# A first softmax rearranged: v transposed under the exponentials, and the A^T W products split into halves by softmax column block

## The chip, the cores and the metric

The kernel runs on one core of one Trainium2 chip. The metric is the device time of one execution in microseconds (us). A kernel is timed in several executions, interleaved with executions of the kernel before on the same chip.

Names in the profiles: PE is TensorE's matmuls, PEld its weight loads, DVE is VectorE, ACT ScalarE, POOL GpSimd, SP SyncE; L282 is line 282 of that kernel. `x6` counts instructions; what stands in square brackets is the idle time of the engine before them, and what ended it.

## The reference, cut to what matters

```python
def _attn_ref(q, k, v, tau):            # q, k, v: 4 x 6144 x 256
    qn = q / (norm(q, axis=1) + 1e-06)  # over the 6144 rows
    kn = k / (norm(k, axis=1) + 1e-06)
    s = kn.transpose(0, 2, 1) @ qn / tau      # 256 x 256 per batch
    a = softmax(s, axis=-1)
    return v @ a
def _moe_ref(x, w1, w2, w3, w_out):     # x: 24576 x 256, w1..w3: 256 x 768, w_out: 768 x 256
    h = np.maximum(np.maximum(x @ w1, x @ w2), x @ w3)
    return h @ w_out
```

Since (v A) W = v (A W), the kernel multiplies the small softmax matrix into the three weights once per batch (tile `aw`; called the A^T W products here, because the softmax matrix lies transposed in memory), and v then meets only these: the h matmuls multiply v^T, v transposed, with them. It works on v in 48 chunks of 512 rows, 12 to a batch.

## The kernel before: the parts concerned

Everything below is about the first batch, before the stream of chunks can start. Its softmax is computed from the Gram products, the matmuls of k with q. The exponentials `et` come in two column blocks, j = 0 and j = 1, and each A^T W product is a sum over both. Row sums give the reciprocal `rinv`, which scales each product when ACT or DVE evicts it from PSUM (the matmul accumulator) to SBUF. `htile` takes one of six PSUM banks, `xtile` one of two.

```python
    ps = gram(0)
    warm_ps = htile("warm_ps")
    for i in range(8):                       # keeps TensorE busy while DVE and ACT work
        PE.matmul(warm_ps, lhsT=ident, rhs=warm, start=(i == 0), stop=(i == 7))
    et = softmax_t(*ps)
    aw = alloc_aw()
    rinv = rowsums(et)                       # 4 tiny matmuls, then DVE.reciprocal
    v_transpose_pe(0)                        # 8 PE transposes, ACT's copy, DVE's copy
    aw_part(et, rinv, aw, 0, FT)             # 12 products, 6 evictions
    ...
    def aw_part(et, rinv, aw, fp, w):
        for m in range(3):                   # the three weights
            for ic in range(CC):
                ew = htile("ew_ps")
                for j in range(CC):
                    PE.matmul(ew[:, :w], lhsT=et[:, j, ic * P:(ic + 1) * P], rhs=w_sb[m][:, j, fsl], ...)
                # evicted by ACT and DVE in turn, times rinv
    ...
    load_v(0)                                # queued behind the k and q loads
    for fp in range(d_ff // FT):
        load_w(fp)                           # block 0 of w1, w2, w3, then block 1, then block 2
```

A helper at the end pins the program's order on each engine, so each engine executes in the order of the source.

## Time and profile before

| | us |
|---|---|
| time, median of three runs | 576.76 |
| TensorE busy, of a span of 574.9 | 555.1 |
| the stretch that the change touches (end of the Gram products to the products of the second weight block) | 34.05 to 39.61 |
| TensorE's gaps after 39.61, up to 570 | none |

The prediction shows the lines for these.

### The profile page before, as it was taken

How to read it: one execution, taken by the hardware profiler on the slowest of the kernel's cores; microseconds unless marked ns; L12 is line 12 of the kernel's file. 1: busy time of each engine (PE TensorE's matmuls, PEld its weight loads, DVE VectorE, ACT ScalarE, POOL GpSimd, SP SyncE). 2: the span in 40 equal slices, each digit the busy share in tenths (PEclk: the TensorE clock that was granted, in tenths of full speed). 3: DMA queues.
4: the chain of work that ended last, by engine and by line, in shares of the span. 5: the costliest groups of instructions: out<-in, count | busy, mean ns of one | idle time of the engine just before them, and what ended most of it. 6: DMA issues, size and time to landing. Idle time of an engine off the chain costs nothing.

```text
span 574.9 us, 9325 instructions
## 1 busy us (share of the span) xinstructions
PE 555.1 (97%) x3328; PEld 328.5 (57%) x3328; DVE 406.4 (71%) x627; ACT 307.2 (53%) x530; POOL 227.3 (40%) x235
## 2 busy tenths in 40 slices
PE   3789999999999999999999999999999999999996
PEld 3655555555755555555575555555575555555554
DVE  0048777777577777777748777777848778778774
ACT  1034567677454466776735447767646444444442
POOL 4232257776731028777761006777760000000000
PEclk9999999999999999999999999999999999999999
DMA  9998998885598228977378526788535234322111
GB/s 142 107 144 157 130 178 124 157 133 113 102 118 164 59 66 155 133 152 130 75 131 130 114 75 101 157 131 130 125 84 127 66 82 129 74 91 76 56 73 74
DMA packets 75951, 65.62 MB, mean 114 GB/s; under 512 B 52353, under 2 KB 61953, under 8 KB 75905
## 3 DMA queue, kind: packets, MB, share of 16 engines
q0 software_dynamic: 18928, 26.48, 39.1%
q1 hardware_dynamic: 56832, 38.28, 22.9%
q8 instruction: 26, 0.43, 0.3%
q10 hardware_dynamic: 144, 0.26, 0.1%
q14 instruction: 21, 0.16, 0.1%
HBM read 78.64 MB, written 25.17 MB: 181 GB/s over the span
## 4 chain that ended last, share of the span: by engine, by line
PE 93%; DMA 5%; ACT 0%; DVE 0%; issue 0%; POOL 0%; DVEq 0%; POOLq 0%
PE h_ps L327 65%; PE o_ps L346 21%; DMA q_sb<-in_q_dram 4%; PE gram L235 3%; PE ew_ps L282 3%; DMA k_sb<-in_k_dram 2%; PE o_ps L366 0%; PE gram L178 0%; PE n_ps L216 0%; PE n_ps L218 0%; ACT et L246 0%; PE gram L180 0%; DVE o_sb L372 0%; POOL k_sb L99 0%; DVE scr L253 0%
## 5 line engine op out<-in xcount | busy, mean ns | idle before, releaser
L327 PE MATMUL h_ps<-vt_sb,aw_sb 128*128 128x512 bf16 x1728 | 406.6, 379 | 0.0
L331 DVE TENSOR_TENSOR s_mx<-h_ps,s_mx 128x512 bf16<-128x512 f32 x288 | 197.9, 687 | 98.1 <-ACT s_mx L330 97.1
L327 PEld LDWEIGHTS <-aw_sb 128*128 128x128 bf16 x1728 | 168.2, 98 | 163.0 <-DVE aw_sb L288 3.7
L330 ACT ACTIVATE s_mx<-h_ps 128x512 bf16<-128x512 f32 x288 | 171.4, 595 | 130.7 <-PE h_ps L327 130.7
L332 DVE TENSOR_TENSOR ht_sb<-h_ps,s_mx 128x512 bf16<-128x512 f32 x288 | 199.2, 692 | 30.7 <-PE o_ps L346 0.5
L204 POOL TENSOR_TENSOR acc<-acc,sq 128x768 f32<-128x768 f32 x90 | 147.7, 1651 | 70.7 <-ACT sq L198 70.5
L346 PE MATMUL o_ps<-wo_sb,ht_sb 128*128 128x256 bf16 x1128 | 153.9, 273 | 0.0
L346 PEld LDWEIGHTS <-ht_sb 128*128 128x128 bf16 x1128 | 110.4, 98 | 52.9
L349 ACT ACTIVATE o_sb<-o_ps 128x512 f32<-128x512 f32 x94 | 56.1, 597 | 83.1 <-PE o_ps L346 83.1
L110 POOL DMA_DIRECT2D v_sb<-in_v_dram x48 | 26.8, 562 | 88.5 <-DMA vt_sb<-v_sb 86.6
L198 ACT ACTIVATE sq<-q_sb 128x768 bf16<-128x768 fp8e4 x48 | 40.5, 844 | 0.0
L198 ACT ACTIVATE sq<-k_sb 128x768 bf16<-128x768 fp8e4 x48 | 40.1, 835 | 0.0
L201 POOL CAST acc<-sq 128x768 f32<-128x768 bf16 x6 | 4.9, 821 | 64.6 <-ACT sq L198 64.6
L102 POOL DMA_DIRECT2D q_sb<-in_q_dram x32 | 17.7, 555 | 10.7 <-DMA k_sb<-in_k_dram 9.7
L166 PE MATMUL kk<-k_sb 128*128 128x256 fp8e4 x48 | 7.8, 339 | 11.7 <-DVE k_sb L152 5.4
L285 ACT ACTIVATE aw_sb<-ew_ps,rinv 128x384 bf16<-128x384 f32 (+1 forms) x27 | 14.4, 546 | 5.7 <-PE ew_ps L282 4.8
L282 PE MATMUL ew_ps<-w_sb,et 128*128 128x384 bf16 (+1 forms) x108 | 17.1, 308 | 0.0
L235 PE MATMUL gram<-k_sb,q_sb 128*128 128x512 fp8e4 x144 | 16.8, 277 | 0.0
L99 POOL DMA_DIRECT2D k_sb<-in_k_dram x29 | 16.0, 554 | 1.0 <-POOLq L462 0.8
L235 PEld LDWEIGHTS <-q_sb 128*128 128x256 fp8e4 x144 | 15.9, 136 | 0.6
L178 PE MATMUL gram<-k_sb,q_sb 128*128 128x512 fp8e4 x48 | 10.7, 323 | 3.4 <-DMA q_sb<-in_q_dram 3.4
L166 PEld LDWEIGHTS <-k_sb 128*128 128x256 fp8e4 x48 | 6.5, 182 | 12.8 <-DMA k_sb<-in_k_dram 6.3
(52 smaller groups left out, 103.6 us busy)
## 6 DMA issues: line engine op xcount, KB each, us to landing
out_dram<-o_sb SPq DMA_DIRECT2D x47, 512.0 KB, 2.8
v_sb<-in_v_dram POOLq DMA_DIRECT2D x48, 256.0 KB, 3.7
k_sb<-in_k_dram POOLq DMA_DIRECT2D x24, 192.0 KB, 5.3
q_sb<-in_q_dram POOLq DMA_DIRECT2D x24, 192.0 KB, 6.8
k_sb<-in_k_dram POOLq DMA_DIRECT2D x5, 256.0 KB, 10.8
q_sb<-in_q_dram POOLq DMA_DIRECT2D x5, 256.0 KB, 19.4
w_sb<-in_moe_w_dram POOLq DMA_DIRECT2D x9, 128.0 KB, 5.7
kf<-in_k_dram SPq DMA_DIRECT2D x2, 512.0 KB, 4.3
```

The lines of the kernel that those rows point to most:

```text
L102: POOL.dma_start(out=qk[b][0][:, g0:g0 + w, :], in_=q_r[b][:, g0:g0 + w, :])
L110: POOL.dma_start(out=t, in_=v_r[gi // NCH, gi % NCH])
L198: ACT.activation(out=sq, in_=src, func=AF.Square)
L204: POOL.tensor_tensor(out=acc, in0=acc, in1=sq, op=ALU.add)
L235: PE.matmul(g[:, j * C:(j + 1) * C], lhsT=qt[:, tsl, j * P:(j + 1) * P], rhs=kt[:, tsl, :], start=(tp == 0 and j == 0), stop=(tp == NG // ...
L282: PE.matmul(ew[:, :w], lhsT=et[:, j, ic * P:(ic + 1) * P], rhs=w_sb[m][:, j, fsl], start=(j == 0), stop=(j == CC - 1))
L327: PE.matmul(t.rearrange("p (t n) -> p t n", t=TPC), lhsT=aw[m][:, ic, fsl], rhs=vt[:, :, ic, :], start=(ic == 0), stop=(ic == CC - 1))
L330: ACT.activation(out=s_mx, in_=hp[0], func=AF.Copy)
L331: DVE.tensor_tensor(out=s_mx, in0=hp[1], in1=s_mx, op=ALU.max)
L332: DVE.tensor_tensor(out=ht[:, fc, :], in0=hp[2], in1=s_mx, op=ALU.max)
L346: PE.matmul(st["ps"][:, half], lhsT=ht[:, fc, t * P:(t + 1) * P], rhs=wo_sb[:, fc, :], start=(fc == 0), stop=(fc == FC - 1))
L349: ACT.activation(out=st["o"][:, t - 1:t + 1, :].rearrange("p t d -> p (t d)"), in_=st["ps"], func=AF.Copy)
```

## The change

The intent: transposes need only v, so they can run while ACT computes the exponentials; and the first half of every product needs only the first exponential, so it can run while ACT computes the second.

```diff
+    def aw_first(et, aw):
+        ...
+        products(0)              # j = 0: six products, two for each weight
+        sums(0)
+        sums(1)
+        DVE.reciprocal(out=rinv, in_=rs_ps[:, 0:CC])
+        products(1)              # j = 1: six products
+        # six evictions, ACT and DVE in turn, as before
...
+        DVE.tensor_copy(out=vt[:, half:, :], in_=ps[:, half:, :])
         ACT.activation(out=vt[:, :half, :], in_=ps[:, :half, :], func=AF.Copy)
-        DVE.tensor_copy(out=vt[:, half:, :], in_=ps[:, half:, :])
...
-    for i in range(8):
-        PE.matmul(warm_ps, lhsT=ident, rhs=warm, start=(i == 0), stop=(i == 7))
+    for i in range(6):
+        PE.matmul(warm_ps, lhsT=ident, rhs=warm, start=(i == 0), stop=(i == 5))
     et = softmax_t(*ps)
+    v_transpose_pe(0)
     aw = alloc_aw()
-    rinv = rowsums(et)
-    v_transpose_pe(0)
-    aw_part(et, rinv, aw, 0, FT)
+    rinv = aw_first(et, aw)
```

More of the change, by code (lines that the diff above doesn't have):

```diff
@@ L290, in aw_part, with sums, products @@
                 n += 1
+    def aw_first(et, aw):
+        rinv = sm.tile([P, CC], FP32, name="rinv")
+        rs_ps = xtile("rs_ps")
+        parts = [(m, ic, htile("ew_ps")) for m in range(3) for ic in range(CC)]
+        def sums(j):
+            for ic in range(CC):
+                PE.matmul(rs_ps[:, ic:ic + 1], lhsT=et[:, j, ic * P:(ic + 1) * P], rhs=ones_c,
+                          start=(ic == 0 and j == 0), stop=(j == CC - 1), skip_group_check=True)
+        def products(j):
+            for m, ic, ew in parts:
+                PE.matmul(ew[:, :FT], lhsT=et[:, j, ic * P:(ic + 1) * P], rhs=w_sb[m][:, j, 0:FT],
+                          start=(j == 0), stop=(j == CC - 1))
+        products(0)
[3 more added lines that the diff above has]
+        products(1)
+        for n, (m, ic, ew) in enumerate(parts):
+            if n % 2 == 0:
+                ACT.activation(out=aw[m][:, ic, 0:FT], in_=ew[:, :FT], func=AF.Copy, scale=rinv[:, ic:ic + 1])
+            else:
+                DVE.tensor_scalar_mul(out=aw[m][:, ic, 0:FT], in0=ew[:, :FT], scalar1=rinv[:, ic:ic + 1])
+        return rinv
     vts = {}
```

## The prediction

> **What bounds the kernel now.** I read the page first: its busy shares, then the chain that ended last.
>
> ```profile
> PE 555.1 (97%) x3328; PEld 328.5 (57%) x3328; DVE 406.4 (71%) x627; ACT 307.2 (53%) x530; POOL 227.3 (40%) x235
> ...
> PE 93%; DMA 5%; ACT 0%; DVE 0%; issue 0%; POOL 0%; DVEq 0%; POOLq 0%
> ```
>
> TensorE is 93% of the chain, the opening loads another 5%. Second I cut the span into stretches at the points that the change touches (columns: stretch, its length, busy time and instructions of PE, PEld, DVE, ACT, POOL; clock; DMA share and GB/s).
>
> ```profile
> 0.00:34.05 34.05, 19.01 (x147) 17.13 (x147) 1.63 (x6) 3.14 (x4) 13.17 (x27) 1.00 1.01 126
> 34.05:39.61 5.56, 5.32 (x40) 2.96 (x39) 3.06 (x12) 3.60 (x9) 2.39 (x4) 1.00 1.44 194
> 39.61:51.44 11.83, 11.83 (x68) 6.44 (x66) 11.09 (x20) 6.88 (x13) 3.18 (x6) 1.00 0.68 109
> 51.44:570.00 518.56, 518.56 (x3077) 301.83 (x3076) 389.93 (x590) 292.99 (x503) 208.54 (x199) 1.00 0.59 113
> ```
>
> Up to 34.05 us the Gram products wait for q and k. From 39.61 us to 570 TensorE has no gap at all: 11.83 of 11.83 and 518.56 of 518.56 us. So only one thing can change: the moment, 39.61 us, at which TensorE has got through the first softmax and the first h block and goes on without a gap. All of the change is in the 5.56 us before it. Third, the timeline of that stretch (start, duration, engine, line, count):
>
> ```profile
> 34.05 1.90 PE L380 MATMUL warm_ps<-warm,ident 128*128 128x512 bf16 x8
> ...
> 35.33 0.91 ACT L246 ACTIVATE et<-e_in,rq 128x256 bf16<-128x256 f32 x2
> ...
> 36.29 0.23 PE L270 MATMUL rs_ps<-ones_c,et 128*128 128x1 bf16 x3 [0.22 <-ACT et L246]
> ...
> 36.38 0.61 PE L312 MATMUL vt_ps<-ident,v_sb 128*128 128x128 bf16 x8
> 36.55 0.17 DVE L272 RECIPROCAL rinv<-rs_ps 128x2 f32<-128x2 f32 x1 [1.06 <-PE rs_ps L270]
> ...
> 36.82 1.47 PE L282 MATMUL ew_ps<-w_sb,et 128*128 128x256 bf16 x12
> 37.02 0.60 ACT L316 ACTIVATE vt_sb<-vt_ps 128x512 bf16<-128x512 bf16 x1 [0.79 <-PE vt_ps L312]
> 37.52 1.20 ACT L285 ACTIVATE aw_sb<-ew_ps,rinv 128x256 bf16<-128x256 f32 x3
> 37.65 0.42 DVE L317 COPY vt_sb<-vt_ps 128x512 bf16<-128x512 bf16 x1 [0.93 <-ACT vt_sb L316]
> 37.99 1.26 DVE L288 TENSOR_SCALAR aw_sb<-ew_ps,rinv 128x256 bf16<-128x256 f32 x3
> ...
> 38.13 1.65 PE L327 MATMUL h_ps<-vt_sb,aw_sb 128*128 128x512 bf16 x6
> ```
>
> A group's duration holds a tail of its last matmul, so I use spacings: warm (1.90-0.38)/7 = 0.22 us, transposes (0.61-0.22)/7 = 0.056, A^T W products (1.47-0.27)/11 = 0.109. The six h matmuls would need 6 x 0.216 = 1.30 us; they take 39.61-38.13 = 1.48, because DVE's first product eviction comes late (37.99), behind its copy of v^T, which itself waited 0.93 us for ACT's copy.
>
> **What the Trainium skill says.** "PSUM — Partial Sum Buffer", section "PSUM bank collisions raise a hardware error", says two engines may not touch one bank in the same quadrant at once, ScalarE with VectorE reads included, so a scheduler orders them. The trace agrees: the two v^T copies read disjoint halves of one bank and run one after the other (0.60, then 0.42 us). Changing their order does not make them parallel. "TensorE: Matmul & The Clock Gate", section "Back-to-back issue gap", gives 262 cycles for 256 columns; at its 2.4 GHz that is 0.109 us, my spacing above. The same page, "What's actually happening" under Part 1, puts the throttle behind an idle window of some 3.4 us; the granted clock is 1.00 in every stretch above, and no gap that I work out below exceeds 0.5 us, so two warm matmuls less should not cost clock. "DMA: Bandwidth & Descriptors", section "Issuing engines are not separate DMA queues", says that all loads interleave on the same 16 DMA engines: so weights that are queued behind q cannot be hurried. The DMA share of 1.44 in the stretch agrees that these are full.
>
> **The change, part by part.**
> (a) Two warm matmuls go: TensorE is free of them at 34.05 + 6 x 0.216 = 35.35 instead of 35.78. This was time in which it waited for the exponentials anyway.
> (b) The eight transposes fill it: 35.35 to 35.79, results complete about 36.0. Their bank is free (the first e_in product ends about 35.16), and v landed about 20.89 + 13.8 = 34.7. They no longer stand, 0.44 us, between sums and products.
> (c) DVE copies its half at about 36.0 to 36.42, ACT its at 36.45 to 37.05. Before, this pair was over at 38.08, in the way of the evictions.
> (d) First-half products need only the first exponential. The first row sum before started at 35.89, just when that exponential was there; so do they now: weight 1 at 35.89 and 36.00, weight 2 at 36.11 and 36.22. Weight 3 would be due at 36.33. Here I looked at when the weights land; the issues of w1 to w3 start at 23.34, 25.80 and 28.25:
>
> ```profile
> 28.25 0.70 POOL L136 DMA_DIRECT2D w_sb<-in_moe_w_dram  x1 [1.73 <-DMA q_sb<-in_q_dram]
> ```
> ```profile
> w_sb<-in_moe_w_dram POOLq DMA_DIRECT2D x1, 128.0 KB, 8.4
> ```
>
> The same view, window by window, gives 12.0, 10.2 and 8.4 us to landing: 35.34, 36.00, 36.65. In the kernel before the third was not wanted until 36.82 + 8 x 0.109 = 37.69, a full 1.0 us of slack, so no wait shows. **In the changed kernel the third weight is wanted 0.32 us before it lands**, and everything behind it on the in-order TensorE (row sums, second half) waits. It starts about 0.05 us after landing, as the late Gram products did after their q (31.27 to 31.32 in the chain in order of time): 36.70 and 36.81, free at 36.92.
> (e) Four row sums, 0.03 us apart, complete about 37.17; the reciprocal, 0.17, at 37.21 to 37.38. It was done at 36.73 before: **the reciprocal comes 0.65 us later**. Second-half products issue at 37.02 to 37.68.
> (f) Evictions start at about 37.42 on both engines. From the rows above: ACT's come 0.36 us apart and last 0.48, DVE's 0.39 and 0.48. ACT ends at 37.90, 38.26, 38.62; DVE at 37.92, 38.31, 38.70.
> (g) h matmuls, each after its weights with 0.04 us for the semaphore, at least 0.216 apart: 37.94, 38.16, 38.37, 38.59, 38.80, 39.02; TensorE is free at 39.24. The evictions stay ahead, so 1.30 us, not 1.48.
> Sum: 39.61 - 39.24 = 0.37 us less. The six PSUM buffers serve as before, since the first h tiles take banks whose evictions they wait for anyway.
>
> **What becomes of it later.** TensorE has no gap after, so 0.37 us should reach the end, unless a load now comes late. The closest is the output weight: issued at 45.16, 5.2 us to landing, so 50.3; wanted at 51.44 before, at 51.07 after. Its issue hangs on the DMA transpose of the second v, which no moved instruction starts. 0.7 us of slack remain. The second column block of the weights lands by about 38.7 and is wanted at 39.24. So 576.76 - 0.37 = 576.4 us.
>
> **The rivals.**
> 1. *No wait for the third weight* (it lands earlier in the timed runs, or my landing sum is wrong). Then first halves are over at 36.55, the reciprocal at 37.0, evictions start at 37.08 (ACT is then held by its v^T copy), h at 37.60, free at 38.90: 0.71 us less, 576.05. Against it: three landings 0.66 us apart on full DMA engines, untouched by the change.
> 2. *The wait eats the gain*: were the weight 0.4 us later, near 37.05, all of (d) to (g) would slip by as much: 576.76, nothing won.
> 3. *Something later gives it back*: the output weight or a v transpose on the DMA queue becomes the wait. 0.7 us of slack speaks against it; it would make 576.7.
> 4. *The clock*: two warm matmuls less leave TensorE throttled. It has 1.00 and is not idle for long; a loss would be several us, 580. Very unlikely.
>
> **Range and chances.** The main line with small errors gives 576.2 to 576.6, the first rival 576.0, the second and third 576.8; the three runs before agree to the hundredth, so spread between runs adds little, a tenth or two. I take 575.8 to 576.9. Two per cent are 11.5 us, more than twice the whole 5.56 us stretch that is changed: faster than that is impossible by this route, slower only by a throttled clock.
>
> **What would show it right or wrong.** Right: in the changed profile TensorE's products show an idle of 0.3 to 0.5 us released by the load of w_sb, between the fourth and fifth; the reciprocal starts about 37.2; the first h matmul at 37.9 and the six without gaps; the next products at about 39.2; no gap after. Wrong: products run through from 35.9 (rival 1); h starts after 38.1 (rival 2); the first o_ps product (line 374 of the changed kernel) waits for wo_sb (rival 3); a granted clock below 1.00 (rival 4).

## More of the kernel before

Most fast runs of one kernel lie within a few tenths of a microsecond of each other; some, of 577.1 to 578.4 us, are longer and still count as fast.

One more view is needed for the comparison: the chain of work that ended last, in order of time (start, length, what). This is its part in the stretch:

```profile
35.33 0.92 ACT et L246 x2
...
36.29 0.23 PE rs_ps L270 x3
36.52 0.47 PE vt_ps L312 x8
36.98 1.31 PE ew_ps L282 x12
38.30 0.22 PE h_ps L327
38.51 0.01 issue
38.52 1.25 PE h_ps L327 x5
39.78 1.31 PE ew_ps L282 x12
```

Exponentials, row sums, transposes, products and h matmuls stand one behind another. The chain puts a matmul's end at the end of its pipeline; the timeline puts the start of the products that follow at 39.62. This start, "TensorE's next products" below, is the moment that each variant is judged by, because TensorE has no gap after it.

## The result and the profile after

The changed kernel took 576.55 us (median of six runs, 576.35 to 576.66), beside 576.80 for the kernel before (six runs, 576.76 to 576.92). The ratio is 0.9995, with a 95% interval of 0.9982 to 1.0008: the interval holds 1. Ratios here are over the fast runs, and not quite the ratio of the medians quoted. A second set on another chip gave 576.67 against 576.69 (ratio 0.9994). So the medians say: between nothing and 0.3 us less, inside the noise. The trace says more.

The page after, its busy line and its chain by engine:

```profile
PE 554.6 (97%) x3325; PEld 327.9 (57%) x3326; DVE 406.7 (71%) x627; ACT 307.3 (53%) x530; POOL 227.2 (40%) x235
...
PE 93%; DMA 6%; issue 0%; DVE 0%; DVEq 0%; POOLq 0%
```

ACT has gone from the chain, and DMA has 6% instead of 5%. The stretches after, cut where TensorE's next products now start and as much later as before (columns as in the prediction):

```profile
39.40:51.23 11.83, 11.83 (x68) 6.46 (x67) 11.09 (x20) 6.88 (x13) 3.17 (x6) 1.00 0.66 108
51.23:569.80 518.57, 518.57 (x3077) 301.75 (x3076) 390.07 (x590) 292.98 (x503) 208.50 (x199) 1.00 0.59 113
```

The same work without a gap, 0.21 us earlier, at a clock of 1.00: nothing was given back later. The 0.21 is that of one profile. In it the first exponential already starts 0.08 earlier than in the kernel before (35.25 for 35.33), which the change did not bring; in the profile of the second set, next products start at 39.52, only 0.10 earlier. From the first exponential on, it is 4.15 us to next products in both, against 4.29 before. So the trace gives 0.1 to 0.2 us. The timeline of the stretch itself:

```profile
35.28 0.61 PE L340 MATMUL vt_ps<-ident,v_sb 128*128 128x128 bf16 x8
...
35.82 0.69 PE L305 MATMUL ew_ps<-w_sb,et 128*128 128x256 bf16 x4
35.93 0.42 DVE L344 COPY vt_sb<-vt_ps 128x512 bf16<-128x512 bf16 x1 [0.51 <-PE vt_ps L340]
36.39 0.60 ACT L345 ACTIVATE vt_sb<-vt_ps 128x512 bf16<-128x512 bf16 x1 [0.23 <-DVE vt_sb L344]
...
36.81 0.38 PE L305 MATMUL ew_ps<-w_sb,et 128*128 128x256 bf16 x2 [0.31 <-DMA w_sb<-in_moe_w_dram]
...
37.30 0.17 DVE L311 RECIPROCAL rinv<-rs_ps 128x2 f32<-128x2 f32 x1 [0.95 <-PE rs_ps L300]
37.57 1.20 ACT L315 ACTIVATE aw_sb<-ew_ps,rinv 128x256 bf16<-128x256 f32 x3 [0.58 <-PE ew_ps L305]
...
38.10 1.47 PE L355 MATMUL h_ps<-vt_sb,aw_sb 128*128 128x512 bf16 x6 [0.15 <-DVE aw_sb L317]
...
39.40 0.82 PE L282 MATMUL ew_ps<-w_sb,et 128*128 128x256 bf16 x6
```

The transposes are over early, four products run, and then TensorE stands still for the load of the third weight. The row sums wait behind that load, the reciprocal behind them, and the evictions behind the reciprocal. The chain in order of time tells it in one piece:

```profile
28.17 8.60 DMA w_sb<-in_moe_w_dram
36.77 0.04 issue
36.81 0.38 PE ew_ps L305 x2
37.19 0.09 PE rs_ps L300 x4
...
37.30 0.18 DVE rinv L311
```

A weight load that the chain of the kernel before did not contain now sets the start of everything.

A smaller wait stands ahead of this one, and no list of waits has it, since it is hidden behind the modelled end of the matmul before. A narrower window splits the four products:

```profile
36.13 0.38 PE L305 MATMUL ew_ps<-w_sb,et 128*128 128x256 bf16 x2
```

The third product, the first with the second weight, starts at 36.13; by the spacing of 0.109 it was due at 36.04, 0.08 earlier by unrounded times. The second weight was issued at 25.72 and landed 10.36 us later, at 36.08, so 0.04 before this start, as the third weight did before the fifth product (36.77 and 36.81).

### The profile page after: what moved, and what is told of

Same layout as the page of the kernel before. It is cut to its first block, busy times and chain, and to the rows that moved or that the text cites. A ratio compares the mean times of both kernels' runs of the same rounds, so it can differ in the third digit from the quotient of the medians.

```text
span 574.7 us, 9320 instructions
## 1 busy us (share of the span) xinstructions
PE 554.6 (97%) x3325; PEld 327.9 (57%) x3326; DVE 406.7 (71%) x627; ACT 307.3 (53%) x530; POOL 227.2 (40%) x235
## 4 chain that ended last, share of the span: by engine, by line
PE 93%; DMA 6%; issue 0%; DVE 0%; DVEq 0%; POOLq 0%
PE h_ps L355 65%; PE o_ps L374 21%; DMA q_sb<-in_q_dram 3%; PE gram L235 3%; PE ew_ps L282 2%; DMA w_sb<-in_moe_w_dram 1%; DMA k_sb<-in_k_dram 1%; PE o_ps L394 0%; PE n_ps L216 0%; PE n_ps L218 0%; DVE o_sb L400 0%; DVE aw_sb L317 0%; PE ew_ps L305 0%; PE rs_ps L270 0%; DVE rinv L311 0%
## 5 line engine op out<-in xcount | busy, mean ns | idle before, releaser
L285 ACT ACTIVATE aw_sb<-ew_ps,rinv 128x384 bf16<-128x384 f32 (+1 forms) x24 | 13.2, 555 | 5.7 <-PE ew_ps L282 4.8
L282 PE MATMUL ew_ps<-w_sb,et 128*128 128x384 bf16 (+1 forms) x96 | 15.6, 313 | 0.0
```

## The experiments

The theory: the landing of the third weight holds the in-order TensorE, so the order of the products undoes most of what the transposes win. The main rival: the gain is small because the v^T copies and evictions bound the stretch anyway. "Next products" is TensorE's start after the first h block, 39.62 before and 39.40 after.

| kernel | next products, us | from the first exponential, us | fast runs, median us | kernel before, same rounds |
|---|---|---|---|---|
| changed kernel, again | 39.52 | 4.15 | 576.67 | 576.69 |
| third weight's products last | 38.90 | 3.49 | 575.95 | 576.75 |
| no third weight (wrong) | 38.89 | 3.68 | 576.08 | 576.75 |
| eight warm matmuls | 39.39 | 4.15 | 576.54 | 576.75 |
| transposes alone | 38.97, again 39.07 | 3.65, again 3.65 | 576.10, again 576.11 | 576.75, 576.69 |
| third weight loaded later | 40.22 | 4.88 | 577.20 | 576.69 |
| transposes alone, ACT copies first | 41.08 in a late run | 3.85 | 576.18 | 576.69 |
| products alone | 40.52 | 5.11 | 577.33 | 576.79 |
| two banks | 38.66 in a slow run | 3.37 | 575.7 (three runs) | 576.79, 576.84 |
| two banks, k and q loads later | 38.54 | 3.36 | 575.69 | 576.57 |

The middle column takes out what the opening loads shift from run to run: it is the start of next products less that of the first exponential (4.29 in the kernel before). The 95% interval of the ratio to the kernel before lies below 1 for the third weight's products last (0.9965 to 0.9996), no third weight, the transposes alone (both times) and two banks in its five rounds, and holds 1 for all the others, the losses included; these rest on the traces and the medians.

**The third weight's products last** (e1).

```diff
-        products(0)
+        products(0, (0, 1))          # the first two weights
         sums(0)
         sums(1)
         DVE.reciprocal(out=rinv, in_=rs_ps[:, 0:CC])
-        products(1)
+        products(1, (0, 1))
+        products(0, (2,))
+        products(1, (2,))
```

> The third weight's four products moved behind the row sums, the reciprocal and the second half of the first two weights. Theory (the load of the third weight holds the in-order TensorE and with it the reciprocal): no wait for w_sb, reciprocal at about 36.6 us instead of 37.3, first eviction about 37.0 (ACT's v^T copy ends then), first h matmul about 37.55, next products at about 38.85 instead of 39.40; time about 0.55 us below the changed kernel, so near 576.0. Rival (the products wait costs nothing because the evictions are bound by the v^T copies on ACT and DVE anyway): next products stay at 39.3 to 39.4, time 576.5.

Its timeline:

```profile
36.78 0.17 DVE L313 RECIPROCAL rinv<-rs_ps 128x2 f32<-128x2 f32 x1 [0.27 <-PE rs_ps L300]
37.05 1.20 ACT L319 ACTIVATE aw_sb<-ew_ps,rinv 128x256 bf16<-128x256 f32 x3
```

As the theory has it: no wait for a load, the reciprocal 0.5 us earlier, next products at 38.90. Fast runs took 575.88 to 576.02, 0.8 us below the kernel before. Three of its six runs were slow (601 to 602 us); more on that below. From the first exponential on it takes 3.49 us, 0.16 less than the transposes alone (3.65, below), and 0.15 by the medians. So dividing the products into halves can pay, if the row sums, on which the evictions hang, come early. In the changed kernel they stand behind all six first halves, and there it wins nothing even without the wait for the third weight (3.68 in the next experiment).

**No third weight** (e2; the result is wrong).

```diff
-                PE.matmul(ew[:, :FT], ..., rhs=w_sb[m][:, j, 0:FT],
+                PE.matmul(ew[:, :FT], ..., rhs=w_sb[min(m, 1)][:, j, 0:FT],
```

> The third weight's products of the first column block read the second weight instead: a wrong result on purpose, same instructions and order. Theory: the 0.31 us idle of TensorE is gone, the first half is through at about 36.45, reciprocal about 36.75, evictions from about 37.0, next products at about 38.85 to 38.9, time near 576.0. Rival (something else than this load holds the reciprocal): idle and 39.4 stay.

The same instructions in the same order, without the wait for that one load:

```profile
35.77 0.90 PE L305 MATMUL ew_ps<-w_sb,et 128*128 128x256 bf16 x6
```

All six products ran through. Next products came at 38.89 and the median was 576.08. This takes away the suspected cause and nothing else; the wait for the third weight cost 0.5 us (39.40 less 38.89, and 4.15 less 3.68 from the first exponential). That is more than the 0.31 us of idle in the changed kernel's profile, because idle is counted from the modelled end of the fourth product; by the issue spacing the fifth was due at 35.82 + 4 x 0.109 = 36.26 and started at 36.81, 0.55 later. Of this, 0.08 was the wait for the second weight, which e2 still has (its six products would take 0.27 + 5 x 0.109 = 0.82 without), and 0.47 the wait for the third.

**Eight warm matmuls again** (e3: `range(8)` in place of `range(6)`, the rest as changed).

> Changed kernel with eight warm matmuls instead of six. Theory: the transposes end 0.43 us later, but so much less is waited for the third weight (it lands about 36.8 anyway): the wait goes to about zero, next products stay at 39.4, time the same as the changed kernel within 0.1. Rival (the two warm matmuls are worth their 0.43 us): next products at 39.8, time 0.4 us longer.

```profile
36.15 1.02 PE L305 MATMUL ew_ps<-w_sb,et 128*128 128x256 bf16 x6
```

The products start 0.33 us later and end where they did: the six take 1.02 us, where six without any wait would take 0.82, so 0.2 is left of the waits, where about zero was expected. Next products 39.39, median 576.54. Two warm matmuls more, ahead of the load's landing, cost nothing here.

**The transposes alone** (e4, and once more as e7): six warm matmuls, transposes ahead, DVE's copy first; row sums and products in the old order.

```diff
-    rinv = aw_first(et, aw)
+    rinv = rowsums(et)
+    aw_part(et, rinv, aw, 0, FT)
```

> Only the first part of the change: six warm matmuls, transposes ahead, DVE's copy first; row sums and products in the old order (both halves of a product together, the third weight's last). Theory: the third weight is wanted only at about 36.3 + 8 x 0.109 = 37.2, after it lands, so no wait; reciprocal about 36.5, first evictions about 37.0 when ACT's v^T copy ends, next products at about 38.85; 0.5 us or more below the changed kernel, near 576.0. So the products' new order would be a loss. Rival (the new order of the products brings part of the gain): next products later than 39.4, time above 576.5.

> The kernel with the transposes moved alone once more, on this chip, as what the act-first kernel is compared with and to see whether the slow runs come back: fast runs at 576.1; if the slow state near 600 us belongs to the edit, again about one run in six or more, and none for the others of this call.

```profile
36.37 1.47 PE L282 MATMUL ew_ps<-w_sb,et 128*128 128x256 bf16 x12
37.68 1.46 PE L355 MATMUL h_ps<-vt_sb,aw_sb 128*128 128x512 bf16 x6
```

In the old order the third weight is wanted last, at 36.37 + 8 x 0.109 = 37.24, after it has landed. Twelve products run through, and h follows on the last of them without a gap. Next products 38.97 and 39.07, fast medians 576.10 and 576.11, some 0.6 us below the kernel before on both chips. Half of the change gives more than the whole.

**The products alone** (e8): the new product order in the kernel before, with eight warm matmuls and the transposes after the row sums, ACT's copy first.

```diff
-    rinv = rowsums(et)
-    v_transpose_pe(0)
-    aw_part(et, rinv, aw, 0, FT)
+    rinv = aw_first(et, aw)      # with v_transpose_pe(0) between the reciprocal and products(1)
```

> The other part alone: eight warm matmuls, first-half products first as in the changed kernel, but the transposes left where they stood, after the row sums, with ACT's copy first. Theory: the third weight is waited for as in the changed kernel (fifth product at about 36.8 us), row sums over at 37.15, transposes at 37.15 to 37.6, second halves at 37.6 to 38.25, ACT's v^T copy at 37.85 to 38.45, DVE's at 38.45 to 38.9 and its three evictions after that, so the first h matmuls end late: next products at about 40.3, time 0.7 us longer than the kernel before, 577.4. Rival (the new product order brings something by itself): next products below 39.6, time below 576.7.

```profile
36.96 0.38 PE L306 MATMUL ew_ps<-w_sb,et 128*128 128x256 bf16 x2 [0.29 <-DMA w_sb<-in_moe_w_dram]
...
39.03 1.65 PE L357 MATMUL h_ps<-vt_sb,aw_sb 128*128 128x512 bf16 x6 [0.49 <-DVE vt_sb L347]
```

The same wait, and then v^T is late as well. Next products 40.52, median 577.33 beside 576.79: with the transposes where they stood, the product order costs 0.5 us by the medians and 0.9 by the trace, whose run, of 577.69, was the longest of the five.

**The third weight loaded later** (e5): in the changed kernel, the second block of the first weight is issued ahead of the third weight's first block.

```diff
-    for fp in range(d_ff // FT):
-        load_w(fp)
+    for fp, i in ((0, 0), (0, 1), (1, 0), (0, 2), (1, 1), (1, 2)):
+        load_w1(fp, i)
+    load_w(2)
```

> Changed kernel with the third weight's first block issued one place later (the second block of the first weight goes ahead of it). It lands then at about 37.5 us instead of 36.8. Theory (everything from the third weight's products to the end hangs on this landing): idle before the fifth product about 1.0 us instead of 0.3, next products about 40.1 instead of 39.4, time about 0.7 us longer than the changed kernel, 577.2. Rival (some slack is left behind this wait): clearly less than 0.7.

```profile
37.62 0.38 PE L310 MATMUL ew_ps<-w_sb,et 128*128 128x256 bf16 x2 [1.03 <-DMA w_sb<-in_moe_w_dram]
```

The load lands at 37.58 by the chain, 0.81 us later than in the changed kernel's profile, and next products come at 40.22, 0.82 later. The fast median is 577.20, 0.53 longer than the changed kernel on the same chip, so less than the 0.7 foretold; its profiled run took 577.34, 0.67 longer than the profiled one of the changed kernel, in which the load had landed at 36.88, so 0.70 earlier. The medians leave it open whether some 0.2 of slack is left; the traces show none behind this landing: in the four profiles with the changed order (changed kernel twice, e3, e5), next products follow it by 2.63 or 2.64 us each time.

**ACT's copy first** (e6): e4 with the two v^T copies in the old order.

> The transposes moved alone, as in the experiment of that name, but ACT copies its half of v^T ahead of DVE, as in the kernel before. Theory (on one bank the two copies must follow each other, and the reciprocal stands behind DVE's copy): ACT copies at 36.2 to 36.8, DVE at 36.85 to 37.25, the reciprocal ends at 37.45 instead of 36.7, evictions from 37.5, next products about 39.3 instead of 38.95, time 0.35 us longer than with DVE first, about 576.5. Rival (the order of the copies does not matter once the transposes are early): 38.95 and 576.1.

This expectation was a miss. The fast median was 576.18 (four of the five runs between 576.14 and 576.25), only 0.07 above the kernel with DVE first on the same chip. Its profile fell in the remaining run, of 578.18 us, whose Gram products ended 1.9 us later at a mean clock of 0.95 in the first 36 us; so I compare from the start of the first exponential: 37.23 to 41.08 is 3.85 us, against 35.42 to 39.07, 3.65 us, with DVE first. So 0.2 by this trace and 0.07 by the medians, not 0.35: I had left out that the kernel with DVE first is bound by its twelve products (36.47 + 12 x 0.109 = 37.78, and h starts at 37.77), so that the evictions there have some slack, and that ACT's copy begins while its last exponential still runs (38.04, and the exponential ends at 38.14). The order of the copies is the smallest part of the change.

**Two banks** (e9, and again e10): e1 with the transposes in two PSUM banks, so that the two v^T copies may run side by side, and the row sums after three first-half products.

```diff
-        vt_ps = xtile("vt_ps", cols=TPC * C, dtype=BF16)
+        pss = [xtile("vt_ps", cols=TPC * C // 2, dtype=BF16) for _ in range(2)]
```

> The third-last order taken further: the v^T transposes go to two PSUM banks, so that DVE and ACT copy at the same time, and the row sums stand after three first-half products. Theory: ACT's v^T copy runs straight after the exponentials, 36.2 to 36.8, instead of behind DVE's; row sums at about 36.35, reciprocal over at 36.85, evictions from 36.95, TensorE through with the products at 37.45, h from there, next products at about 38.75; time 0.15 us below the third-last kernel, 575.8. The first output product is then wanted at about 50.55, as the output weight lands (50.4 to 50.5): from here on that load is the next limit. Rival (bank conflict or the product stream bounds it already): 38.9 and 575.95 as in the third-last kernel.

> The two-bank kernel once more, because its profile fell in a run of 1517 us that is of no use. As expected there: in a fast run ACT's v^T copy at 36.2 to 36.8 beside DVE's, evictions from 36.95, next products at about 38.75, first output product at about 50.55, time 575.6 to 575.9. Rival: 38.9 as in the third-last kernel.

The three fast runs took 575.59, 575.71 and 575.87. Both profiles fell in slow runs, one of 1517 us, in which TensorE was slow before any instruction that differs and whose stretch says nothing, and one of 590 us. In the latter, the stretch up to 40 us is undisturbed (clock 1.00 up to 80 us): ACT's copy starts at 36.10, just before DVE's ends (35.74 to 36.16); next products at 38.66, the first output product at 50.48, 0.08 us after the output weight landed. The third product, and with it the row sums, waits for the second weight here (landed at 36.13, start at 36.18), so that load is a limit as well. The two edits, banks and place of the row sums, were not tried apart. But later TensorE stands still. From the list of waits of that run (who waits, for what: us in total, times, longest), then its busy time in 80 to 95 us:

```profile
PE h_ps L360 <- DMA vt_sb<-v_sb: 9.5, 2, 4.8
```
```profile
80.00:95.00 15.00, 10.30 (x59) 5.60 (x58) 8.59 (x13) 7.06 (x12) 11.29 (x11) 0.92 1.21 89
```

TensorE waits twice, 4.7 and 4.8 us, for v transposes on the DMA queue, and its clock is lower (0.92 in this stretch). The four transposes issued between 57 and 95 us took 17.9 to 29.6 us to land, against 3.3 to 19.2 in the profile of the kernel before.

**Two banks with the k and q loads later** (e11).

```diff
-            if more and 1 <= ch < 9:
-                load_k(b + 1, (ch - 1) * 6, 6)
-                load_q(b + 1, (ch - 1) * 6, 6)
+            if more and 2 <= ch < 10:
+                load_k(b + 1, (ch - 2) * 6, 6)
+                load_q(b + 1, (ch - 2) * 6, 6)
```

> The two-bank kernel with the k and q loads of the next batch begun one chunk later (chunks 2 to 9 instead of 1 to 8), because in its profiled slow run of 590 us TensorE waited twice, 4.7 and 4.8 us, for v transposes that took up to 29 us to land in a stretch from 57 to 125 us where loads and transposes were in flight together. Theory (the slow runs of 590 to 605 us are this pile-up of transfers): with one k and q pair less in the burst after 57 us the transposes land earlier and no run of the six is slow, where five of eight were; fast runs at 575.7 as before. Rival (the slow runs have another cause, such as the chip's own state): about half the runs are again near 600 us.

Transposes issued between 57 and 95 us, from issue to landing (min, median, max):

```profile
DMA to landing us min/median/max: 3.3/5.3/15.1
```

None of five runs was near 600 us; three took 575.63 to 575.69, two 577.43 and 577.44. Next products came at 38.54. Its median is 0.88 us below the kernel before (576.57 in the same rounds), the lowest of all medians here by 0.02, though the two longer runs put the ratio at 1.00 (0.9986 to 1.0013), so that it is faster is not shown. If the slow runs had come at the two-bank kernel's rate of five in eight, five runs without one would have a chance of under 1%. But the run of 1517 us is one of the five, each set ran on another chip, and the rate changed from set to set for one and the same kernel (e4 one of six, e7 none of five). That the load order prevents slow runs is not shown.

**What stays open.** Runs of 590 to 605 us occurred in e1 (three of six), e4 and e7 (one of eleven), e5 (one of five) and two banks (four of eight, besides the one of 1517), and in none of 49 runs of the kernel before or 11 of the changed one. One of them was profiled, and there it was late v transposes. That this is so in the others, and that an earlier TensorE brings it about, is not shown: e5 is later than the kernel before and had one too. No comparison above uses a slow run's time; the start times of two banks are those of a slow run's undisturbed opening. The runs of 577.4 to 578.4, in e6, e11 and the kernel before alike, were not traced to a cause either, apart from the late Gram products in e6's.

## Why the prediction was right, point by point

- **The bound and the size of the stretch**: right. TensorE has no gap after the stretch before or after, and the change moved only the stretch.
- **(a), (b), (c), warm matmuls, transposes, copies**: right. Transposes from 35.28 (35.35 foretold), DVE's copy at 35.93, ACT's at 36.39 behind it (36.0 and 36.45). All is some 0.07 early, as the first exponential is in this profile.
- **(d) The third weight**: right, and the heart of it. Four products from 35.82, then an idle of 0.31 us, released by the load of w_sb, between the fourth and the fifth. By start times the wait is 0.47 us, where 36.70 - 36.33 = 0.37 was foretold. The load landed at 28.17 + 8.60 = 36.77 instead of 36.65: it was issued 0.08 earlier and took 0.2 longer. Over the profiles with an undisturbed opening and the old load order, its landing lay between 36.67 and 36.93; why it varies was not traced. That the loads cannot be hurried was not tried, and a DMA share of 1.44 does not show it: above 1, it counts packets that overlap. The prediction missed the second weight: it let it land at 36.00, 0.11 before its use, and in the changed kernel it landed at 36.08, 0.04 after its products were due. That this did no harm is luck, since the third weight came later still.
- **(e), (f) Reciprocal and evictions**: right in mechanism. The reciprocal started at 37.30 (37.21); the evictions at 37.57 (37.42). The term mis-sized was the hop from the end of the reciprocal to the first eviction: I had taken 0.04 us, and it measured 0.1 (37.47 to 37.57).
- **(g) h matmuls**: without gaps as foretold, six in 39.40 - 38.10 = 1.30 us.
- **The sum**: 0.37 us foretold, 0.21 by the first trace and 0.10 by the second, next products at 39.40 and 39.52 for 39.24. The 0.16 of the first is the later landing (0.11 to the start of the fifth product) and the longer hop (0.05); in the second the load landed 0.11 later still. The time, 576.55 for 576.4, lay in the range, but the range of 575.8 to 576.9 held rivals 1 to 3 and no gain at all too, and the medians of the second set differ by 0.02. So the time tells little; the named wait in the trace, between the fourth and fifth product, is what bears the prediction out.
- **The rivals**: rival 1 is what e2 and e1 made, next products at 38.9 and times near 576.0, so its size was right too and its absence from the changed kernel is shown. Rival 2 is e5: a later landing goes straight to the end. Rivals 3 and 4 did not occur: the output weight was not waited for and the clock was 1.00. The two-bank kernel shows how near rival 3 was: there the output weight lands only 0.08 us before its use.

What the prediction did not ask is which half of the change was worth having. By the medians the transposes alone win 0.6 us and the products alone lose 0.5; of both together, 0.1 to 0.2 remains by the traces.

## What to carry to other kernels

Before a use of loaded data is moved forward, put its new time beside the landing time of the load: a load with 1.0 us of slack showed no wait in the profile before, and moving its first use 1.4 us forward made it the start of the critical chain. Where an engine executes in the order of the source, as here, the order of independent work should follow the order in which its operands land, and work that others depend on (here the row sums) should stand ahead of work that waits for a load. Test the parts of a change alone, since one of them can be paying for the other.

## What the Trainium skill lacked or had wrong

- "TensorE: Matmul & The Clock Gate", section "Back-to-back issue gap", says that in a stream of weight loads and matmuls the spacing at 512 columns is about 131 ns, and that the isolated formula over-counts there. Here the stream of h matmuls, each with its own weight load, is spaced 216 ns, which is the isolated formula's value (518 cycles at 2.4 GHz), and the 256-column products 109 ns.
- "Perfetto Trace Analysis", section "Optimization Strategy", looks for gaps and what ends them. It lacks this: a wait that is absent says nothing of the slack behind it (1.0 us for the third weight in the kernel before, a wait of 0.31 us in the changed one).
- I found no page that says how far the landing of a transpose on the DMA queue spreads when loads are in flight beside it. Here those issued from 57 to 95 us took 3.3 to 19.2 us to land in the kernel before, and 17.9 to 29.6 us in one slow run.
